# Threshold attention and a SoLU feed-forward block on one core: other places for the loads of q, k and v, and one more place for weights times v

## The chip, the core and the metric

The kernel runs on one core of one Trainium2 chip. The metric is device time in microseconds (us); 13 executions of the kernel before had a median of 925.93 us, from 922.73 to 934.3. Five engines work side by side, each through its own list of instructions in order: TensorE (PE in the profile; PEld is its weight load), VectorE (DVE), ScalarE (ACT), GpSimd (POOL) and SyncE (SP), which issues DMAs. They wait for each other through semaphores.

## The reference

First an attention for 8 batches and 8 heads, with 576 rows of 64 columns each, in float32. Scores more than tau under their row's maximum are put out of play before the softmax:

```python
scores = scale * np.matmul(q, k.transpose(0, 1, 3, 2))
thresh = np.max(scores, axis=-1, keepdims=True) - tau
scores = np.where(scores >= thresh, scores, -1000000000.0)
scores = scores - np.max(scores, axis=-1, keepdims=True)
attn = np.exp(scores)
attn = attn / (np.sum(attn, axis=-1, keepdims=True) + 1e-09)
return np.matmul(attn, v).astype(np.float32)
```

Its result, seen as x with 4608 tokens of 512 columns, goes through a feed-forward block: `h = x @ w_in` (1024 columns), `solu = h * softmax(h)`, a layer norm of solu with gain `g_ln`, and `@ w_out` (back to 512 columns).

## The kernel before

The kernel is one long list that a Python loop writes at build time. The loop counts **rounds** (`rnd`). In the first 144 rounds (NS) each does one **slot**: the scores of 128 query rows for two heads, 18 slots per batch (PER = 18). Sixteen of the 18 are for the first 512 rows, two at a time for a pair of heads; the last two are for the 64 rows at the end ("ends") of every head. Rounds after 144 finish what is left.

**What a round holds, in the order in which it is written.** Loads due in this round (`load_at`); copies of finished output (`begin`); the turning of q and k pieces for later heads (`preps`, TensorE transposes of up to 7 pieces of 64 columns, copied out by ScalarE and VectorE) and the scores (line 391); the row maxima with tau (line 408, VectorE, twice a round); the ramp that drops what is under the threshold (line 419, ScalarE); the exponentials (line 428, ScalarE). Then, for the slot before, the division by the sum (line 438, GpSimd); the feed-forward's vector steps (`middle`); one feed-forward step on TensorE, and perhaps weights times v; the turning of the weights in 32 x 32 blocks for the slot before (line 450, VectorE), and after every second slot, in an even round, four DMAs that bring them into the order that TensorE needs (wT<-T, line 461); at last `late`, more feed-forward steps and the store of out (line 669).

**The scores' two PSUM tiles, s0 and s1,** are written anew each round, so TensorE can begin a round's scores only when the ramp and the copies of the round before have read them.

**Weights times v (PV,** `attend`, line 486) is due three rounds after the second slot of its pair. It takes one of two PSUM tiles, p0 and p1, which the feed-forward uses too. When the attention of 256 tokens is complete, two units of 128 tokens are put on the list `ready`.

**The feed-forward** of a unit takes four steps on TensorE, one a round: h halves 0 and 1 (line 540), later o halves 0 and 1 (line 642). `quarter` counts them: 0 and 1 are h of unit `cur`, 2 and 3 are o of the unit before it, `prev`. In quarter 2 the loop passes through an o step even where there is no `prev`; that round's step is then empty. After h half 1 (round n) come the maximum and exponential (n), the product (n+1), the statistics and norm (n+2), in the middle of round n+3 the **swap**, four DMAs from SP of 64 KB each that exchange 32-row groups between u and V (V<-u, line 620), and in round n+4 `ff_turn` on VectorE (uT<-V, line 630), which waits for the swap. The next round's row maxima stand behind `ff_turn` in VectorE's list.

**Where PV is placed** is decided by one condition, which lets it run beside no feed-forward step or an h step, never beside an o step:

```python
due = bool(pv_due) and pv_due[0][0] <= rnd
if due and (step is None or step[0] == "h") and len(pairs_free) > (step == ("h", 0)):
    attending = pv_due.pop(0)[1]
```

**Loads.** A batch's q, k and v come in halves of four heads. `load_qk` loads q and k of a half (512 KB each) and with half 0 the ends of all heads (two DMAs of 128 KB); `load_v` loads v of a half in five DMAs, once in order (512 KB), once with the two halves of the partitions exchanged (2 x 256 KB), and the last 64 rows twice (2 x 64 KB). For batch b > 1, with r = 18(b-1), they stand at the start of rounds r+2 (q and k, half 0), r+8 (half 1), r+9 (v, half 0) and r+24 (v, half 1); for batch 1 at 8, 12, 15 and 24. q and k have two buffers each, v three. All go through SP's queue, like the wT, swap and store DMAs, in the order in which they are written. SP waits for whatever the next DMA in its list needs, and the others stand behind it.

In the first 16 rounds the feed-forward's weights are loaded and decoded as well (`weight_load`, `weight_a`, `weight_b`, `weight_d`), in rounds 0, 2 and 4 whole pairs of heads are turned.

Of the kernel before, what the change touches and what calls it, by code (L numbers as in the profile page):

```python
# [8 lines left out]
F32 = mybir.dt.float32  # L9
# [7 lines left out]
P = 128  # L17
# [3 lines left out]
def kernel(  # L21
# [27 lines left out]
    nc = tc.nc  # L49
    B, H, S, D = q.shape  # L50
    DM, DFF = w_in.shape
    SM = 512
# [35 lines left out]
    NK = S // 64  # L88

    halves = {}  # L90
    ends = {}
# [6 lines left out]
    pairs_free = ["p0", "p1"]  # L98
# [17 lines left out]
        )  # L116


    def load_qk(b, hf):
        d = halves.setdefault((b, hf), {})  # L120
        hs = slice(4 * hf, 4 * hf + 4)

        if hf == 0:
            ends[b] = loads.tile([P, H, D], F32, tag="ends", name="ends")
        for nm, src, rows in (("q", q, ROWS[0]), ("k", k, ROWS[1])):
            d[nm] = loads.tile([P, 4, 4, D], F32, tag=nm, name=nm)

            parts = [slice(0, 2), slice(2, 4)] if b == 0 and hf == 0 else [slice(0, 4)]
            for x, part in enumerate(parts):
                queue = nc.scalar if nm == "k" and x + 1 < len(parts) else nc.sync  # L130
                queue.dma_start(
                    out=d[nm][:, part].rearrange("p h t d -> p h (t d)"),
                    in_=src[b, hs, 0:SM, :][part].rearrange("h (p t) d -> p h (t d)", t=4),
                )
                if hf == 0 and x == 0:
                    queue.dma_start(
                        out=ends[b][rows], in_=src[b, :, SM:S, :].rearrange("h p d -> p h d")
                    )

    def load_v(b, hf):  # L140
        d = halves.setdefault((b, hf), {})
        hs = slice(4 * hf, 4 * hf + 4)


        d["v"] = loads.tile([P, 4, NK, D], F32, tag="v", bufs=3, name="v")
        rest = v[b, hs, 0:SM, :].rearrange("h (p t) d -> p h (t d)", t=4)
        for to, rows, of in (
            (0, slice(0, P), slice(0, P)), (4, ROWS[0], ROWS[1]), (4, ROWS[1], ROWS[0])
        ):
            nc.sync.dma_start(  # L150
                out=d["v"][rows, :, to : to + 4].rearrange("p h t d -> p h (t d)"), in_=rest[of]
            )
        for rows in ROWS:
            nc.sync.dma_start(
                out=d["v"][rows, :, NK - 1], in_=v[b, hs, SM:S, :].rearrange("h p d -> p h d")
            )
# [285 lines left out]
    def blocks(s):  # L442
        b, kind, hp, r = slots[s]
        key = (b, kind, hp)
        if r == 0:
            units[key] = dict(T=work.tile([P, NB, 2, 2, 32], F32, tag="T", name="T"))
        u = units[key]
        T = u["T"]
        for h, w in enumerate(live.pop(s)["w"]):
            nc.vector.transpose(out=T[:, :, r, h, :], in_=w)  # L450
        if r == 0:
            return

# [222 lines left out]
    PER = NS // B  # L676
# [22 lines left out]
    load_at = {}  # L699
    for b in range(1, B):  # L700
        r = PER * (b - 1)

        for at, job, hf in zip(
            (2, 8, 9) if b > 1 else (8, 12, 15), (load_qk, load_qk, load_v), (0, 1, 0)
        ):
            load_at.setdefault(r + at, []).append(lambda b=b, job=job, hf=hf: job(b, hf))
        load_at.setdefault(r + PER + 6, []).append(lambda b=b: load_v(b, 1))

    with tc.manual_schedule():
        load_qk(0, 0)  # L710
        nc.scalar.dma_start(out=tau_t, in_=tau.partition_broadcast(P))
        constants()
        for x in range(3):
            weight_load(x)
        load_qk(0, 1)
        load_v(0, 0)
        nc.sync.dma_start(out=g_rows, in_=g_ln.rearrange("(c p) -> c p", p=P))
        whole_pair(0)
# [2 lines left out]

        pieces = {r: x for x, r in enumerate(range(16))}
        whole = {0: 1, 2: 2, 4: 3}
        load_at[3] = [lambda: load_v(0, 1)]

        ready = []
        rnd = 0
# [7 lines left out]
        while True:  # L735
            more = rnd < NS
            if not more and not (
# [1 line left out]
                or max([rnd - 1, *begin, *middle, *late]) >= rnd  # L739
            ):  # L740
                break
            for job in load_at.pop(rnd, []):
                job()
            for job in begin.pop(rnd, []):
                job()
            if rnd == NS:
# [39 lines left out]
            due = bool(pv_due) and pv_due[0][0] <= rnd  # L786
            step = None
            if quarter < 2 and cur is not None:
                step = ("h", quarter)
            elif quarter == 3:  # L790
                step = ("o", 1)
            elif not more:
                if between and ffn[between[0]].get("turned", NS + rnd) <= rnd:
                    prev = between.pop(0)
                    step = ("o", 0)
            elif quarter == 2 or (prev is not None and not due):
                if prev is None or (ffn[prev].get("turned", NS + rnd) <= rnd and w2_done):
                    step = ("o", 0)

            attending = None  # L800
            if due and (step is None or step[0] == "h") and len(pairs_free) > (step == ("h", 0)):
                attending = pv_due.pop(0)[1]
            if step == ("h", 0):
                ff_h(cur, 0, rnd + 1 < NS)
# [1 line left out]
            elif step == ("h", 1):  # L806
# [8 lines left out]
                at = rnd + 4 if more or not ready else rnd + 6  # L815
# [24 lines left out]
            if rnd - 1 in live:  # L840
                blocks(rnd - 1)
            for job in late.pop(rnd, []):
                job()
            if rnd == 3:
                gains()
            if rnd in pieces:
                x = pieces[rnd]
# [42 lines left out]
```

## Time and profile before

| | us |
|---|---|
| median of 13 executions | 925.93 |
| the profiled execution | 929.29 |
| its span (first to last instruction of the program) | 927.5 |
| TensorE busy | 858.1 (93%) |
| VectorE busy | 678.8 (73%) |
| ScalarE busy | 591.6 (64%) |
| GpSimd busy | 451.7 (49%) |
| a wT DMA (288 of 288 KB), issue to landing, median | 5.8 |
| a swap DMA (144 of 64 KB) | 4.0 |
| q and k loads (15 each of 512 KB) | 6.2 and 7.1 |
| v loads (16 of 512 KB) | 8.4 |
| all that the DMAs moved | 154.61 MB, 167 GB/s in the mean |

The profile is of one execution. Rows of engines in 40 slices give the busy share of each slice in tenths (9 is 90% or more); PEclk is the share of its full clock that TensorE was granted. In lists of waits a row says which engine and line waited for which, then the total in us, the number of times and the longest. In a timeline a row has start and duration in us, engine, line and operation, and in brackets how long the engine had been idle and what ended that; "issue" there means that the profile shows nothing that the engine waited for. "SPq" is SP issuing a DMA.

### The profile page before, as it was taken

How to read it: one execution, taken by the hardware profiler on the slowest of the kernel's cores; microseconds unless marked ns; L12 is line 12 of the kernel's file. 1: busy time of each engine (PE TensorE's matmuls, PEld its weight loads, DVE VectorE, ACT ScalarE, POOL GpSimd, SP SyncE). 2: the span in 40 equal slices, each digit the busy share in tenths (PEclk: the TensorE clock that was granted, in tenths of full speed). 3: DMA queues.
4: the chain of work that ended last, by engine and by line, in shares of the span. 5: the costliest groups of instructions: out<-in, count | busy, mean ns of one | idle time of the engine just before them, and what ended most of it. 6: DMA issues, size and time to landing. Idle time of an engine off the chain costs nothing. (4 is left out here: it accounts for less than half of the span.)

```text
span 927.5 us, 39657 instructions
## 1 busy us (share of the span) xinstructions
PE 858.1 (93%) x17089; PEld 623.5 (67%) x17089; DVE 678.8 (73%) x1306; ACT 591.6 (64%) x1240; POOL 451.7 (49%) x870
## 2 busy tenths in 40 slices
PE   5567779989899999999999999989999999999997
PEld 3335457868777777767777667866667777676555
DVE  5898967768867877767867777767867777877352
ACT  5766656767756766666767676757757677776121
POOL 2535545536555555545545555545545455655120
PEclk8778799999999999999999999999999999999999
DMA  8899868975879557975879557965878655866412
GB/s 255 202 246 254 188 133 190 234 173 127 181 167 225 129 133 179 232 160 133 187 148 226 129 130 181 228 143 129 187 171 209 139 130 128 189 144 143 91 47 47
DMA packets 95470, 154.61 MB, mean 167 GB/s; under 512 B 27192, under 2 KB 69184, under 8 KB 95296
## 3 DMA queue, kind: packets, MB, share of 16 engines
q1 hardware_dynamic: 93920, 150.12, 70.2%
q8 instruction: 134, 2.20, 1.0%
q10 hardware_dynamic: 1376, 1.97, 0.6%
q14 instruction: 40, 0.33, 0.1%
HBM read 46.14 MB, written 9.44 MB: 60 GB/s over the span
## 5 line engine op out<-in xcount | busy, mean ns | idle before, releaser
L408 DVE CUSTOM_DVE_ANT_0 w<-s_ps,tau_t 128x576 f32<-128x576 f32 x288 | 206.5, 754 | 154.3 <-PE s_ps L391 129.6
L419 ACT ACTIVATE w<-s_ps,nth 128x576 f32<-128x576 f32 x288 | 207.5, 743 | 122.2 <-DVE nth L408 98.4
L642 PE MATMUL o_ps<-w,uT 64*64 64x256 f32 x4608 | 272.1, 380 | 8.7 <-DVE uT L630 7.7
L642 PEld LDWEIGHTS o_ps<-w,uT 64*64 64x64 f32 x4608 | 218.1, 134 | 72.2 <-issue 24.4
L540 PE MATMUL h_ps<-w,xh 64*64 64x512 f32 x1856 | 221.6, 595 | 5.3 <-issue 5.3
L438 POOL TENSOR_SCALAR w<-w,sm 128x576 f32<-128x576 f32 x288 | 218.1, 769 | 14.3
L428 ACT ACTIVATE w<-w,ntau 128x576 f32<-128x576 f32 x288 | 220.3, 772 | 0.0
L450 DVE STREAM_TRANSPOSE T<-w 128x576 f32<-128x576 f32 x288 | 205.7, 750 | 4.4 <-POOL w L438 4.2
L486 PEld LDWEIGHTS pv<-wT,v 64*64 64x64 f32 x5760 | 171.0, 138 | 45.2 <-issue 25.4
L391 PE MATMUL s_ps<-kT,qT 64*64 64x64 f32 (+1 forms) x2048 | 174.2, 425 | 25.1 <-ACT w L419 22.8
L486 PE MATMUL pv<-wT,v 64*64 64x128 f32 (+1 forms) x5760 | 175.0, 266 | 10.1 <-DMA wT<-T 6.9
L540 PEld LDWEIGHTS h_ps<-w,xh 64*64 64x64 f32 x1856 | 111.6, 134 | 98.4 <-issue 68.0
L435 POOL TENSOR_SCALAR sm<-sm 128x2 f32<-128x2 f32 x144 | 35.7, 248 | 278.5 <-ACT w L428 275.7
L436 POOL TENSOR_TENSOR sm<-sm,mone 128x2 f32<-128x2 f32 x144 | 107.1, 744 | 12.0
L391 PEld LDWEIGHTS s_ps<-kT,qT 64*64 64x64 f32 x2048 | 64.4, 139 | 34.2 <-ACT w L419 28.9
L604 ACT ACTIVATE V<-u,nb,rs 128x1024 f32<-128x1024 f32 x36 | 44.7, 1241 | 53.3 <-POOL nb L594 53.3
L508 ACT COPY xh<-pv 128x256 f32<-128x256 f32 x64 | 23.9, 373 | 75.3 <-PE pv L486 75.3
L630 DVE STREAM_TRANSPOSE uT<-V 128x1024 f32<-128x1024 f32 x36 | 44.1, 1225 | 24.5 <-DMA V<-u 24.2
L428 ACT ACTIVATION_READ_ACCUMULATOR w<-w,ntau 128x1 f32 x288 | 57.0, 198 | 0.0
L562 ACT ACTIVATE u<-h_ps,hm 128x1024 f32<-128x1024 f32 x36 | 40.2, 1118 | 25.0 <-DVE hm L553 19.3
L553 DVE TENSOR_REDUCE hm<-h_ps 128x1 f32<-128x1024 f32 x36 | 43.0, 1194 | 14.0 <-PE h_ps L540 8.0
L568 DVE TENSOR_TENSOR u<-h_ps,u 128x1024 f32<-128x1024 f32 x36 | 42.8, 1189 | 10.4 <-ACT u L562 10.4
(74 smaller groups left out, 607.0 us busy)
## 6 DMA issues: line engine op xcount, KB each, us to landing
wT<-T SPq DMA_DIRECT2D x288, 288.0 KB, 5.8
V<-u SPq DMA_DIRECT2D x144, 64.0 KB, 4.0
out_dram<-ob SPq DMA_DIRECT2D x72, 128.0 KB, 2.8
v<-in_v_dram SPq DMA_DIRECT2D x16, 512.0 KB, 8.4
v<-in_v_dram SPq DMA_DIRECT2D x32, 256.0 KB, 7.7
q<-in_q_dram SPq DMA_DIRECT2D x15, 512.0 KB, 6.2
k<-in_k_dram SPq DMA_DIRECT2D x15, 512.0 KB, 7.1
raw<-in_moe_w_out_dram SPq DMA_DIRECT2D x8, 512.0 KB, 7.9
```

Of the source, the lines that this page charges most:

```text
L391: nc.tensor.matmul(out=ps[h][ROWS[y], ks], lhsT=lhsT, rhs=d["kT"][ROWS[h], ks], start=True, stop=True,)
L408: nc.vector.tensor_tensor_reduce(out=w, in0=ps[:, 0:S], in1=tau_t.to_broadcast([P, S]), scale=1.0, scalar=BIG, op0=ALU.add, op1=ALU.min, a ...
L419: nc.scalar.activation(out=d["w"][x], in_=d["ps"][x][:, 0:S], func=AF.Prelu, bias=d["nth"][x], scale=-1.0, alpha=1.0e30,)
L428: nc.scalar.activation(out=w, in_=w, func=AF.Exp, bias=ntau, scale=1.0, accum_out=sm[:, x : x + 1])
L436: nc.gpsimd.tensor_tensor(out=sm, in0=sm, in1=mone, op=ALU.pow)
L438: nc.gpsimd.tensor_scalar(out=w, in0=w, scalar1=sm[:, x : x + 1], scalar2=1.0, op0=ALU.mult, op1=ALU.mult)
L450: nc.vector.transpose(out=T[:, :, r, h, :], in_=w)
L486: nc.tensor.matmul(out=to, lhsT=d["v"][ROWS[u], h0 + h, m ^ 4 * u if m < 8 else m], rhs=rhs, start=m == 0, stop=m == NK - 1,)
L540: mm = nc.tensor.matmul(out=h[ROWS[y], f], lhsT=x[ROWS[r], c, ROWS[y]], rhs=w1_parts[ROWS[r], c, part ^ r], start=part == 0 and c == 0, st ...
L604: nc.scalar.activation(out=V, in_=u, func=AF.Identity, bias=nb, scale=rs)
L630: nc.vector.transpose(out=uT, in_=d["V"].rearrange("p y (m x) -> p m y x", x=32))
L642: nc.tensor.matmul(out=d["o"][ROWS[z], 512 * r : 512 * r + 256], lhsT=d["uT"][ROWS[r], m].rearrange("p y x -> p (y x)"), rhs=w2[ROWS[r], m ...
```

## The change

Two things change. First, each half's q, k and v are loaded in smaller portions, with a place of their own each: q and k apart (`load_one`), and v in two portions (`load_v` with `parts`: 0 is the 512 KB in order, 1 and 2 are the rest). For batch b > 1, with r = 18(b-1), the places are the ends of rounds r-1 (q, half 0), r+1 (k, half 0), r+7 (k, half 1), r+9 (q, half 1), r+11 and r+13 (v, half 0), r+21 and r+23 (v, half 1). For batch 1 they are 8, 7, 11, 12, 13, 15, 21 and 23. What is due in a round is now written behind the round's `late` steps and no longer ahead of everything; the load of batch 0's second half of v in round 3 moves with it. Whichever of q and k comes first for half 0 allocates the tile for the ends.

Second, up to round 39 PV may also run in a round whose feed-forward step is o half 1. It stands behind that step in TensorE's list.

```diff
-    def load_qk(b, hf):
+    def load_one(b, hf, nm, queue=None):
         d = halves.setdefault((b, hf), {})
         hs = slice(4 * hf, 4 * hf + 4)
-        if hf == 0:
-            ends[b] = loads.tile([P, H, D], F32, tag="ends", name="ends")
-        for nm, src, rows in (("q", q, ROWS[0]), ("k", k, ROWS[1])):
-            d[nm] = loads.tile([P, 4, 4, D], F32, tag=nm, name=nm)
...
+        src, rows = {"q": (q, ROWS[0]), "k": (k, ROWS[1])}[nm]
+        d[nm] = loads.tile([P, 4, 4, D], F32, tag=nm, name=nm)
+
+        parts = [slice(0, 2), slice(2, 4)] if b == 0 and hf == 0 else [slice(0, 4)]
+        for x, part in enumerate(parts):
+            queue = nc.scalar if nm == "k" and x + 1 < len(parts) else nc.sync
+            queue.dma_start(
+                out=d[nm][:, part].rearrange("p h t d -> p h (t d)"),
+                in_=src[b, hs, 0:SM, :][part].rearrange("h (p t) d -> p h (t d)", t=4),
+            )
+            if hf == 0 and x == 0:
+                if b not in ends:
+                    ends[b] = loads.tile([P, H, D], F32, tag="ends", name="ends")
                 queue.dma_start(
+                    out=ends[b][rows], in_=src[b, :, SM:S, :].rearrange("h p d -> p h d")
                 )
...
+    def load_qk(b, hf):
+        load_one(b, hf, "q")
+        load_one(b, hf, "k")
+
+    def load_v(b, hf, parts=(0, 1, 2)):
...
-        d["v"] = loads.tile([P, 4, NK, D], F32, tag="v", bufs=3, name="v")
+        if 0 in parts:
+            d["v"] = loads.tile([P, 4, NK, D], F32, tag="v", bufs=3, name="v")
...
-        for to, rows, of in (
-            (0, slice(0, P), slice(0, P)), (4, ROWS[0], ROWS[1]), (4, ROWS[1], ROWS[0])
+        for part, to, rows, of in (
+            (0, 0, slice(0, P), slice(0, P)), (1, 4, ROWS[0], ROWS[1]), (1, 4, ROWS[1], ROWS[0])
         ):
...
+            if part in parts:
+                nc.sync.dma_start(
+                    out=d["v"][rows, :, to : to + 4].rearrange("p h t d -> p h (t d)"),
+                    in_=rest[of],
+                )
-        for rows in ROWS:
+        for rows in ROWS if 2 in parts else ():
...
-        for at, job, hf in zip(
-            (2, 8, 9) if b > 1 else (8, 12, 15), (load_qk, load_qk, load_v), (0, 1, 0)
+        for at, job, hf, what in (
+            (-1 if b > 1 else 8, load_one, 0, "q"),
+            (1 if b > 1 else 7, load_one, 0, "k"),
+            (7 if b > 1 else 11, load_one, 1, "k"),
+            (9 if b > 1 else 12, load_one, 1, "q"),
+            (11 if b > 1 else 13, load_v, 0, (0,)),
+            (13 if b > 1 else 15, load_v, 0, (1, 2)),
+            (PER + 3, load_v, 1, (0,)),
+            (PER + 5, load_v, 1, (1, 2)),
         ):
-            load_at.setdefault(r + at, []).append(lambda b=b, job=job, hf=hf: job(b, hf))
-        load_at.setdefault(r + PER + 6, []).append(lambda b=b: load_v(b, 1))
+            load_at.setdefault(r + at, []).append(
+                lambda b=b, job=job, hf=hf, what=what: job(b, hf, what)
+            )
...
-        load_at[3] = [lambda: load_v(0, 1)]
+        load_at.setdefault(3, []).append(lambda: load_v(0, 1))
...
-            for job in load_at.pop(rnd, []):
-                job()
             for job in begin.pop(rnd, []):
...
-            if due and (step is None or step[0] == "h") and len(pairs_free) > (step == ("h", 0)):
+            fits = step is None or step[0] == "h" or (rnd < 2 * PER + 4 and step == ("o", 1))
+            if due and fits and len(pairs_free) > (step == ("h", 0)):
                 attending = pv_due.pop(0)[1]
...
             for job in late.pop(rnd, []):
                 job()
+            for job in load_at.pop(rnd, []):
+                job()
```

More of the change, by code (lines that the diff above doesn't have):

```diff
@@ L116, in sync @@
         )
-    def load_qk(b, hf):
+    def load_one(b, hf, nm, queue=None):
         d = halves.setdefault((b, hf), {})
         hs = slice(4 * hf, 4 * hf + 4)
-        if hf == 0:
-            ends[b] = loads.tile([P, H, D], F32, tag="ends", name="ends")
-        for nm, src, rows in (("q", q, ROWS[0]), ("k", k, ROWS[1])):
-            d[nm] = loads.tile([P, 4, 4, D], F32, tag=nm, name=nm)
-            parts = [slice(0, 2), slice(2, 4)] if b == 0 and hf == 0 else [slice(0, 4)]
-            for x, part in enumerate(parts):
-                queue = nc.scalar if nm == "k" and x + 1 < len(parts) else nc.sync
+        src, rows = {"q": (q, ROWS[0]), "k": (k, ROWS[1])}[nm]
[10 more added lines that the diff above has]
+                    ends[b] = loads.tile([P, H, D], F32, tag="ends", name="ends")
@@ L131, in load_qk @@
                 queue.dma_start(
-                    out=d[nm][:, part].rearrange("p h t d -> p h (t d)"),
-                    in_=src[b, hs, 0:SM, :][part].rearrange("h (p t) d -> p h (t d)", t=4),
-                )
[L135 to L140, printed above, removed]
+                    out=ends[b][rows], in_=src[b, :, SM:S, :].rearrange("h p d -> p h d")
+                )
@@ L141, in load_v @@
+    def load_qk(b, hf):
+        load_one(b, hf, "q")
+        load_one(b, hf, "k")
+    def load_v(b, hf, parts=(0, 1, 2)):
         d = halves.setdefault((b, hf), {})
         hs = slice(4 * hf, 4 * hf + 4)
-        d["v"] = loads.tile([P, 4, NK, D], F32, tag="v", bufs=3, name="v")
+        if 0 in parts:
+            d["v"] = loads.tile([P, 4, NK, D], F32, tag="v", bufs=3, name="v")
         rest = v[b, hs, 0:SM, :].rearrange("h (p t) d -> p h (t d)", t=4)
-        for to, rows, of in (
-            (0, slice(0, P), slice(0, P)), (4, ROWS[0], ROWS[1]), (4, ROWS[1], ROWS[0])
-        ):
-            nc.sync.dma_start(
-                out=d["v"][rows, :, to : to + 4].rearrange("p h t d -> p h (t d)"), in_=rest[of]
-            )
```

## The prediction

> **What bounds the kernel now.** I read the page first: TensorE is busy 93% and its clock is low only in the first fifth of the span.
>
> ```profile
> span 927.5 us, 39657 instructions
> PE 858.1 (93%) x17089; PEld 623.5 (67%) x17089; DVE 678.8 (73%) x1306; ACT 591.6 (64%) x1240; POOL 451.7 (49%) x870
> ...
> PE   5567779989899999999999999989999999999997
> ...
> PEclk8778799999999999999999999999999999999999
> DMA  8899868975879557975879557965878655866412
> ```
>
> So a gain has to come out of TensorE's roughly 69 us of idle time, or out of time at half clock. The list of waits says who causes them (total us, times, longest):
>
> ```profile
> DVE uT L630 <- DMA V<-u: 24.2, 13, 5.6
> ...
> PE o_ps L642 <- DVE uT L630: 7.7, 4, 3.4
> ...
> PE pv L486 <- DMA wT<-T: 6.9, 4, 3.2
> ```
>
> Then I put the timeline into rounds: line 408 runs twice a round, so its pairs date the rounds. From round 39 four rounds repeat, one unit's h half 0, h half 1, then another unit's o half 0, o half 1, with weights times v ("PV") beside both h halves. Windows of four rounds (us, then each engine's busy us and count, granted clock, DMA share, GB/s):
>
> ```profile
> 245.20:271.00 25.80, 23.73 (x518) 17.55 (x514) 16.29 (x31) 14.44 (x32) 12.34 (x25) 1.00 0.82 179
> 271.00:293.60 22.60, 22.60 (x477) 18.09 (x472) 17.73 (x35) 15.92 (x35) 11.95 (x25) 1.00 0.90 215
> 385.20:410.90 25.70, 23.59 (x493) 17.65 (x488) 17.84 (x37) 16.08 (x36) 11.95 (x24) 1.00 0.81 185
> 410.90:433.50 22.60, 22.60 (x476) 17.84 (x472) 17.87 (x35) 16.04 (x35) 12.08 (x25) 1.00 0.60 131
> 455.60:482.40 26.80, 24.93 (x516) 18.38 (x512) 17.36 (x31) 15.35 (x31) 13.00 (x27) 0.94 0.76 164
> 598.00:625.00 27.00, 24.40 (x489) 17.36 (x485) 17.96 (x37) 15.86 (x36) 11.63 (x24) 0.94 0.71 153
> 669.70:695.30 25.60, 23.48 (x516) 15.23 (x512) 17.35 (x31) 15.48 (x31) 13.01 (x27) 1.00 0.78 170
> ```
>
> A clean four takes 22.6 us with TensorE never idle; five fours take 25.6 to 27.0. In each of the five a bulk load stands in SP's queue shortly before a swap (V<-u). Round 63 to 64:
>
> ```profile
> 388.48 2.86 SPq L150 DMA_DIRECT2D v<-in_v_dram  x3
> 391.38 1.27 SPq L154 DMA_DIRECT2D v<-in_v_dram  x2
> 392.76 4.66 SPq L620 DMA_DIRECT2D V<-u  x4
> 399.71 1.25 DVE L630 STREAM_TRANSPOSE uT<-V 128x1024 f32<-128x1024 f32 x1 [3.98 <-DMA V<-u]
> 401.10 3.25 PE L642 MATMUL o_ps<-w,uT 64*64 64x256 f32 x56 [0.72 <-DVE uT L630]
> ```
>
> Five loads of v (1.1 MB) are issued just ahead of the swap; VectorE waits 3.98 us for it, in order, so the next round's row maxima, ScalarE behind them and TensorE are late. After the q and k load of round 74 the stall is different: TensorE gets no instructions.
>
> ```profile
> 465.58 0.20 PEld L540 LDWEIGHTS h_ps<-w,xh 64*64 64x64 f32 x7 [2.69 <-issue]
> ...
> 466.50:469.90 3.40, 3.40 (x31) 2.04 (x24) 0.60 (x1) 0.00 (x0) 1.89 (x3) 0.50 0.88 167
> ```
>
> The second line shows what follows: 3.4 us at clock 0.50.
>
> **What the Trainium skill says.** "DMA: Bandwidth & Descriptors", section "Queues, rings and completion order": each DMA engine takes descriptors in ring order, rings of other queues in turn. The trace agrees: the swap above lands only when v has. "Runtime: NRT & Kernel Launch", "Instruction fetch mechanics": instructions come in 16 KiB blocks through a DMA queue of their own, "mostly hidden". Here queue q8 moves 2.20 MB in 134 packets (16 KB each), and 2.69 us was not hidden. "TensorE: Matmul & The Clock Gate", "What's actually happening": idling a window of about 3.4 us halves the clock until a busy window has passed. The trace agrees (0.50 above, and after the idle stretches in rounds 16, 19, 28 and 100).
>
> **The change part by part.**
>
> *Loads.* The same 16 DMAs per batch, same bytes, same SP issues (0.6 to 1.9 us each); no compute instruction is added. Before, they come in lumps of 1.0 to 1.3 MB, at round 18(b-1) plus 2 (q, k half 0), 8 (q, k half 1), 9 (v half 0) and 24 (v half 1), each at the round's start. After, lumps of 0.5 to 0.64 MB stand at the end of odd rounds: plus -1 (q, half 0), 1 (k, half 0), 7 and 9 (k, q, half 1), 11 and 13 (v, half 0), 21 and 23 (v, half 1). Those that move later keep their margin: q of half 1 is turned from round 12 on and v of half 1 first read in round 26, two whole rounds (9 us or more) after their issue, against landings of 6.2 and 8.4 us in the table of issues; were one late, TensorE would wait the difference, some 2 us. I followed the loop by hand to see what stands next to them. The swap is in odd rounds nearly always (from round 76 in those that leave 3 over 4), in the middle, so a load at the end stands behind it and behind the store of out in SP's queue, where it used to stand before both; next comes wT in the even round, issued 3 to 4.5 us into it. At the 215 to 255 GB/s of busy stretches 0.6 MB takes 2.5 us, so it is through.
>
> Saving from round 39 on: the five fours 25.8 + 25.7 + 26.8 + 27.0 + 25.6 - 5 x 22.6 = 17.9 us; smaller excesses by the same subtraction (fours that begin in rounds 55, 79, 91, 95, 119) 0.4 + 0.9 + 0.6 + 1.0 + 1.4 = 4.3. Sum 22.
> Before round 39: in round 16 the swap stands behind v and VectorE waits 5.6 us; TensorE idles 3.4 and loses half of the 3.4 us at half clock that follow: 5.1. Round 30 waits 1.5 for wT, round 28 0.9 for instructions. Round 10 waits 2.9 for wT behind q and k; now q stands behind wT: 1.5. Sum 9.
>
> New SP waits: v half 1 takes the buffer of the previous batch's v half 0, whose last reader is the PV of that batch's row ends. By my walk it runs one round before the load, or in the same round (57, 75, 111). There SP waits until that PV ends, about one PV (2.2 us), and queued behind is only the wT of the even round, 3 us or more away. Cost nothing; if the cover went, up to 2.2 us three times.
>
> *PV in an o's second half, rounds below 40.* No work is added, only order. In the list of steps PV now falls in rounds 14, 18, 22, 26, 32 and 36 and is never overdue there; h and o run up to two rounds ahead, but two rounds without h or o come later (65, 74). From round 75 both kernels have identical steps, so the end is untouched and only the filling of thin rounds counts. TensorE's need per step, from rounds' durations: scores 0.85, h 3.4, o 3.5, PV 2.2, transposes 0.12 per piece.
> Before, thin rounds 14, 19, 28, 29, 38 last 6.7 + 6.3 + 6.5 + 4.8 + 4.5 = 28.8 and carry 1.5 + 3.5 + 3.5 + 3.6 + 3.1 = 15.2: 13.6 lost, less the 0.9 counted above, plus 1.3 of half clock in round 20: 14.0.
> After: round 14, VectorE-bound with the weight decoding, 6.7 - 3.05 = 3.7, its successor 0.4; round 27 has neither PV nor h or o, ScalarE needs 5.5 (ramps and exponentials 3.4, norm 1.24, copies) for 1.55 of TensorE work, 4.0; PV alone in 28, 65, 74: 1.7 + 1.7 + 1.5; h without PV in 19, 23, 29, 33, 37: rounds 21 and 31 show 4.6 against 4.2, so 2.0. Sum 15.0. An o half with PV is not in the trace: at least 4.5 + 2.2 = 6.7 us; above it wT may be late, whose margin in the nearest cases, PV two rounds after wT's issue, is mostly 2 to 3 us, so 0 to 2.3 (a load ahead of it) five times, 0 to 11 us; I take 1. Net 14 - 16 = a loss of 2.
>
> Sum: 22 + 9 - 2 = 29 us. A stall for instructions can come with any backlog, so I take 85%: 25 us. The profiled execution took 929.3 (span 927.5 and 1.8 around it) and becomes 904. The median, 925.9, is 3.4 lower, so a part of the stalls that I subtract was this execution's own; I take 24 from the median: **902 us**.
>
> **The rivals.**
> 1. *Half of it* (0.33). The smaller loads stand right behind wT in rounds without a swap, and backlog still meets instruction fetches. For: such waits follow q, k and v alike. Against: the clean four at 271.00 carries 215 GB/s. Half of 29: 908 to 920.
> 2. *wT late, slower* (0.05). The 25 PVs of every fourth round from 44 start 1.2 to 6.6 us (mostly 2 to 3) after wT's landing, as far as landings are known. If a load (2.5 us) stands ahead of wT, each could wait up to 1.3, and so could the five in an o half. It decides at 29/30 = 1.0 us each; at 1.3 the time is 926 - 29 + 39 = 936. Against: wT is issued 3 us or more into the even round.
> 3. *Hidden anyway* (0.04): SP reaches the new places just as early because it runs ahead of the engines, so transfers collide as before; 924 to 928. Against: the swap precedes the load in SP's order now, whatever SP's lead.
> 4. *More than counted* (0.05): each removed idle stretch also spares a half-clock window; 885 to 892.
>
> **How the numbers follow.** The likeliest, 0.53, is 892 to 908 with 902 inside. Eight in ten: 891 to 916, from most of rival 4's edge to two thirds of rival 1. A measurement of this kernel cannot tell 0.3% (2.8 us) from no change. Faster 0.53 + 0.33 + 0.05 = 0.91, same 0.04, slower 0.05.
>
> **What would show it.** Right: VectorE's wait for V<-u falls from 24.2 to under 6 us; the five fours come to about 22.6; the clock row stays at 9 after the first seven slices; round 27 is thin. Wrong: PV waits for wT over 10 us; TensorE's issue waits unchanged; swaps still issued behind loads (in SP's own list line 620 waits 7.0 us, six times, for v). The prediction fails if fetch stalls move rather than go, or if PV in an o half waits for wT.

## The result, and the profile after

The kernel after takes 910.54 us in the median (11 executions, 906.41 to 916.65) against 925.69 us for the kernel before on the same chips (48 executions). The ratio is 0.9848, 95% interval 0.9822 to 0.9873: 15.2 us faster. The forecast was 902 us, within 891 to 916. The direction and the range held; the likeliest case (892 to 908) was missed by 2.5 us.

The two profiled executions lie further apart than the medians: 929.29 and 907.58 us, 21.7. The page of the kernel after:

```profile
span 905.5 us, 39662 instructions
...
PE 852.7 (94%) x17089; PEld 670.5 (74%) x17089; DVE 678.2 (75%) x1306; ACT 591.7 (65%) x1240; POOL 451.6 (50%) x870
...
PE   5668799999999999999999999999999999999997
...
PEclk9667899999999999999999999999999999999999
DMA  8899886877777777876876777876876756766322
```

TensorE does the same 17089 matmuls. From the sixth slice to the last but one its row holds nothing but 9, where the row before had 7 and 8 for longer and again in between, and the DMA row, which used to swing between 5 and 9, lies mostly at 6 to 8. The deep swings are gone. Two rows from the list of waits of the kernel before (total us, times, longest):

```profile
PEld h_ps L540 <- issue: 75.6, 296, 3.0
...
PEld pv L486 <- issue: 25.4, 78, 2.6
```

The list of the kernel after:

```profile
PEld h_ps L545 <- issue: 43.0, 210, 2.1
...
PEld pv L491 <- issue: 22.3, 56, 4.7
...
DVE uT L635 <- DMA V<-u: 10.0, 10, 4.1
...
PE pv L491 <- DMA wT<-T: 8.6, 7, 3.8
```

VectorE's wait for the swap fell from 24.2 to 10.0 us. Of those 10.0, 6.0 lie behind round 135, where no load is left in either kernel, 4.1 of them in one wait at the very end. The kernel before has 5.7 us there too, so the part that loads could touch fell from 18.5 to 4.0 us. The waits marked "issue" became fewer as well. The timeline shows why the swap is waited for less. This is SP's list in rounds 65 to 67, with the v load that stood ahead of the swap in the lines of round 63 shown before, and then VectorE's line that waits for the swap:

```profile
395.25 3.36 SPq L625 DMA_DIRECT2D V<-u  x4
398.71 1.71 SPq L674 DMA_DIRECT2D out_dram<-ob  x2
400.46 0.59 SPq L154 DMA_DIRECT2D v<-in_v_dram  x1
401.16 4.03 SPq L466 DMA_DIRECT2D wT<-T  x4
```

```profile
401.98 1.25 DVE L635 STREAM_TRANSPOSE uT<-V 128x1024 f32<-128x1024 f32 x1 [0.97 <-DMA V<-u]
```

The swap is issued first, v behind it, and the wait is 0.97 us instead of 3.98. The v loads themselves land in 6.5 us (512 KB, median) instead of 8.4. But the windows of four rounds (us, each engine's busy us and count, granted clock, DMA share, GB/s) that begin in rounds 39, 63, 75, 99 and 111 did not all become clean:

```profile
246.66:269.91 23.25, 23.24 (x450) 18.49 (x453) 17.74 (x34) 15.74 (x34) 12.27 (x25) 1.00 0.78 172
382.73:404.73 22.00, 20.88 (x517) 17.73 (x512) 17.13 (x35) 15.66 (x35) 12.52 (x25) 1.00 0.74 180
...
445.18:469.16 23.98, 23.32 (x518) 17.58 (x514) 16.14 (x31) 14.39 (x32) 12.31 (x25) 1.00 0.73 171
582.83:605.36 22.53, 22.53 (x489) 18.11 (x485) 17.91 (x36) 15.89 (x36) 11.61 (x24) 1.00 0.73 176
...
650.09:674.49 24.40, 23.22 (x516) 16.99 (x512) 17.36 (x31) 15.36 (x31) 12.98 (x27) 1.00 0.73 169
```

The fours of 63 and 99 are short now (25.7 and 27.0 before), though TensorE still idles 1.1 us in the first. Those of 75 and 111 lie 1.4 and 1.8 us above 22.6, where the prediction took 4.2 and 3.0 to go, and in a second profiled execution of the same kernel 2.7 and 3.7 (25.25 and 26.29 us).

**Stages.** The same windows over whole stages, in us, from one profiled execution each. "Loads only" and "PV only" are experiments told below.

| rounds | before | after | after, again | loads only | loads only, again | PV only |
|---|---|---|---|---|---|---|
| 10 to 14 | 28.4 | 29.1 | 25.5 | 27.6 | 25.7 | 28.8 |
| 14 to 39 | 146.1 | 147.5 | 146.0 | 138.5 | 137.8 | 153.4 |
| 39 to 75 | 210.4 | 198.5 | 199.1 | 206.4 | 205.9 | 209.5 |
| 75 to 143 | 396.0 | 384.5 | 387.8 | 390.3 | 390.5 | 396.2 |
| behind 143 | 75.8 | 75.9 | 75.9 | 75.9 | 75.9 | 75.8 |

Rounds 14 to 39 did not gain at all in the kernel after, and 39 to 75 gained 11.9. That is the move of PV: 176 more of the recorded matmuls lie in rounds 14 to 39 (2980 against 2804) and 206 fewer in rounds 39 to 75 (4120 against 4326).

### The profile page after: what moved, and what is told of

Read it like the earlier page. It is cut to its first block, busy times and chain, and to the rows that moved or that the text cites. A ratio compares the mean times of both kernels' runs of the same rounds, so it can differ in the third digit from the quotient of the medians.

```text
span 905.5 us, 39662 instructions
## 1 busy us (share of the span) xinstructions
PE 852.7 (94%) x17089; PEld 670.5 (74%) x17089; DVE 678.2 (75%) x1306; ACT 591.7 (65%) x1240; POOL 451.6 (50%) x870
## 5 line engine op out<-in xcount | busy, mean ns | idle before, releaser
L647 PEld LDWEIGHTS o_ps<-w,uT 64*64 64x64 f32 x4608 | 236.9, 133 | 43.8 <-ACT xh L513 9.7
L545 PE MATMUL h_ps<-w,xh 64*64 64x512 f32 x1856 | 219.3, 589 | 1.8 <-issue 1.8
L455 DVE STREAM_TRANSPOSE T<-w 128x576 f32<-128x576 f32 x288 | 205.9, 751 | 5.5 <-POOL w L443 5.2
L491 PEld LDWEIGHTS pv<-wT,v 64*64 64x64 f32 x5760 | 176.6, 139 | 37.5 <-issue 22.3
L396 PE MATMUL s_ps<-kT,qT 64*64 64x64 f32 (+1 forms) x2048 | 178.8, 423 | 19.7 <-ACT w L424 17.2
L491 PE MATMUL pv<-wT,v 64*64 64x128 f32 (+1 forms) x5760 | 178.8, 268 | 10.6 <-DMA wT<-T 8.6
L545 PEld LDWEIGHTS h_ps<-w,xh 64*64 64x64 f32 x1856 | 125.6, 133 | 77.3 <-issue 43.0
L396 PEld LDWEIGHTS s_ps<-kT,qT 64*64 64x64 f32 x2048 | 70.6, 140 | 29.5 <-ACT w L424 25.1
```

The source lines that it names most:

```text
L396: nc.tensor.matmul(out=ps[h][ROWS[y], ks], lhsT=lhsT, rhs=d["kT"][ROWS[h], ks], start=True, stop=True,)
L491: nc.tensor.matmul(out=to, lhsT=d["v"][ROWS[u], h0 + h, m ^ 4 * u if m < 8 else m], rhs=rhs, start=m == 0, stop=m == NK - 1,)
L545: mm = nc.tensor.matmul(out=h[ROWS[y], f], lhsT=x[ROWS[r], c, ROWS[y]], rhs=w1_parts[ROWS[r], c, part ^ r], start=part == 0 and c == 0, st ...
L647: nc.tensor.matmul(out=d["o"][ROWS[z], 512 * r : 512 * r + 256], lhsT=d["uT"][ROWS[r], m].rearrange("p y x -> p (y x)"), rhs=w2[ROWS[r], m ...
```

## The experiments

My theory was that of the prediction: the new places of the loads carry the gain, PV's move about nothing. The rivals: PV's move helps or hurts by itself; the size of the portions does it, not the place; the q and k lumps cause the stalls for instructions, or something else does.

### Which part carries the gain

Loads only is the kernel after with the old condition for PV:

```diff
-            fits = step is None or step[0] == "h" or (rnd < 2 * PER + 4 and step == ("o", 1))
+            fits = step is None or step[0] == "h"
```

> The new places of all loads, with PV placed as before (never beside an o step). Theory (the loads carry the gain, PV's move is about neutral): ratio to the kernel before 0.980 to 0.988, 907 to 915 us against 925.7; VectorE's wait for V<-u under 12 us. Rival A (PV's new place carries it): 0.995 or more. Rival B (both are needed, because PV's move shifts the swaps by two rounds against the loads): 0.990 to 0.995.

PV only is the kernel before with the new condition:

```diff
-            if due and (step is None or step[0] == "h") and len(pairs_free) > (step == ("h", 0)):
+            fits = step is None or step[0] == "h" or (rnd < 2 * PER + 4 and step == ("o", 1))
+            if due and fits and len(pairs_free) > (step == ("h", 0)):
```

> PV also beside an o's second half below round 40, with all loads where they were. Theory: within 0.4% of before, since only the order of thin rounds changes. The swaps before round 65 then fall on other rounds than the q and k lumps of batch 3, so one stall of about 3 us may go or come. Rival A: 0.980 to 0.988. Its VectorE wait for V<-u stays over 18 us by the theory.

Loads only: 910.3 us, ratio 0.9806 (0.977 to 0.9841). PV only: 931.48 us, 1.0044 (1.0021 to 1.0066), slower. The loads carry all of it, and PV's move alone costs 4 us. The stages of PV only, rounds 14 to 39 and 39 to 75:

```profile
100.91:254.29 153.38, 141.23 (x3000) 107.44 (x3001) 111.51 (x223) 101.55 (x220) 76.92 (x147) 0.97 0.73 164
254.29:463.83 209.54, 201.22 (x4120) 151.82 (x4123) 158.23 (x309) 141.91 (x299) 108.61 (x212) 0.98 0.75 170
```

Rounds 14 to 39 take 7.3 us more than before and rounds 39 to 75 only 0.9 less, although 206 matmuls have left them: with the old loads TensorE idles 8.3 us there, with the new ones 2.3 (198.52 less 196.25 in the kernel after). So what PV's move pays in advance came back only where little else held TensorE up. With the new loads it pays 9.7 and gets back 7.4 by round 75 (after against loads only, again). Behind round 75, where both have the same steps, the kernel after is another 2.5 to 6.0 us shorter in its two profiled executions, nearly all of it in the fours that begin in rounds 75 and 111; why was not taken apart. By the ratios (0.9848, and 0.9795 in a later run, against 0.9806 and 0.9816) PV's move is about neutral.

### Place or size

The first experiment moves v of half 0 (all of its five DMAs) from the start of its round to the end, behind the swap, and leaves all else as before:

```diff
+        load_end.setdefault(r + (9 if b > 1 else 15), []).append(lambda b=b: load_v(b, 0))
...
+            for job in load_end.pop(rnd, []):
+                job()
```

> From the kernel before: one lump of v, half 0 of each batch, still whole (1.1 MB), moved from the start of its round to the round's end, behind the swap. Everything else as before. Theory 'place' (the swap waits for what stands ahead of it in SP's queue): the fours that begin in rounds 63 and 99 fall from 25.7 and 27.0 us to about 22.6 and round 16 from 10.7 to about 6.5, 8 to 12 us in all, ratio 0.987 to 0.992; VectorE's wait for V<-u 24 to about 12 us. Rival 'size' (the lump itself saturates the DMA engines wherever it stands): 0.997 to 1.003.

The second keeps it at the start, ahead of the swap, but splits it as the kernel after does:

```diff
+        for at, parts in ((9, (0,)), (11, (1, 2))):
+            load_at.setdefault(r + at + 6 * (b == 1), []).append(
+                lambda b=b, parts=parts: load_v(b, 0, parts)
+            )
```

> From the kernel before: v, half 0, cut in two portions (0.5 and 0.63 MB) at the starts of rounds r+9 and r+11 (batch 1: 15 and 17), so a portion still stands ahead of the swap in the fours that begin in rounds 63 and 99. Everything else as before. Theory 'place': a portion ahead delays the swap by about 2.5 us, of which some is hidden; the two fours keep a part of their stall, 23.5 to 25.5 us each, ratio 0.992 to 0.997, clearly less gain than the whole lump moved behind the swap (0.9894). Rival 'size': cutting is what helps, both fours come to about 22.6 and the ratio to 0.987 to 0.991, as good as behind the swap or better.

Behind the swap, whole: 917.25 us, 0.9894 (0.9855 to 0.9933). Ahead of the swap, split: 916.22 us, 0.9893 (0.9852 to 0.9934). The fours of 63 and 99, first of the whole load behind the swap:

```profile
386.55:409.85 23.30, 23.30 (x493) 17.46 (x489) 17.91 (x36) 16.42 (x36) 12.15 (x25) 1.00 0.71 182
595.81:620.11 24.30, 23.53 (x488) 16.09 (x484) 17.91 (x37) 17.09 (x37) 12.62 (x26) 1.00 0.82 187
```

then of the split load ahead of it:

```profile
373.12:397.80 24.68, 23.82 (x492) 16.37 (x488) 18.03 (x36) 16.53 (x36) 12.15 (x25) 1.00 0.80 190
...
585.07:607.95 22.88, 22.88 (x492) 16.35 (x488) 18.02 (x36) 16.11 (x36) 11.97 (x24) 1.00 0.86 199
```

Either suffices for about half of the gain. The place cuts VectorE's wait for the swap more (to 12.2 us against 17.3), so the prediction's mechanism is there; but it is not the only way to the same time, and the prediction argued from the place. The split is no pure test of size, though: one DMA of 512 KB is left ahead of the swap, and the other four go to a round without a swap.

What SP may issue belongs to this. In the kernel before, the swap's fourth DMA was issued at 396.91 us, just after the first v DMA had landed at 396.89, and the two DMAs of the store at 397.67 and 398.48, after the second and third (397.61 and 398.46). Each is the eighth behind the one that it follows. In all fourteen profiles no DMA of SP was issued before the one eight places ahead of it had landed, as far as landings are known. So five DMAs of v ahead of the swap also take places that its four need. Whether this limit is the chip's or that of the program as built was not tested.

### q and k

Only q and k get their new portions and places; v is as before.

> From the kernel before: q and k alone get their new places, one at a time; v's loads and PV stay. Theory: the fours that begin in rounds 39, 75 and 111, where the lump of q, k and ends stood two DMA groups ahead of a swap and of a block of TensorE's instructions, fall from 25.8, 26.8 and 25.6 us to 22.6 to 24, 6 to 10 us in all, ratio 0.989 to 0.994; v's stalls in rounds 16, 64 and 100 stay. Rival (q and k never mattered, v did): 0.998 to 1.002.

920.93 us, 0.992 (0.9889 to 0.9951). The wait for the swap stays (26.5 us), and so do the two fours that v spoils:

```profile
379.93:406.77 26.84, 24.95 (x493) 19.00 (x489) 17.94 (x36) 16.13 (x36) 11.97 (x24) 0.94 0.75 174
...
591.50:618.49 26.99, 24.48 (x488) 16.91 (x484) 17.94 (x37) 15.84 (x36) 11.62 (x24) 0.94 0.73 172
```

The fall to 22.6 to 24 us that I had expected for the fours of 39, 75 and 111 did not come: they take 24.2, 26.1 and 24.9. What q and k gain is spread: 0.5 to 1.7 us each in the fours that begin in rounds 14, 18, 39, 55, 75, 79, 91, 111 and 119, while those of 26, 30 and 63 take 0.5, 1.7 and 1.1 longer. The two savings, 1.06% for v's first half and 0.80% for q and k, make 1.86%, of loads only's 1.94%. They add as far as the intervals tell (each is 0.6 to 0.8% wide), which fits two separate causes.

### What is left when there are no loads

This kernel is loads only without the loads of batches 1 to 7; every batch is computed with batch 0's q, k and v, so only the transfers and their issuing are missing, no instruction of an engine that computes.

```diff
-            load_at.setdefault(r + at, []).append(
-                lambda b=b, job=job, hf=hf, what=what: job(b, hf, what)
-            )
+            pass
```

> The kernel with the new places of the loads and PV as before, but with the loads of batches 1 to 7 left out (35 MB); every batch computes with batch 0's q, k and v. It shows what loads can cost at most. Theory 1 (what is left after the change in the fours that begin in rounds 75 and 111, 27.0 and 26.9 us, is a stall for TensorE's instructions that does not come from loads but from the dense list of PV for the row ends, 144 matmuls with their weight loads, followed by h and a PV): both fours stay over 25 us and the ratio is 0.970 to 0.980. Theory 2 (loads near by cause it): both fall to about 22.6 and the ratio is 0.960 to 0.970.

The lines show only the core of the edit; the places that look up q, k and v ask for batch 0's. 907.74 us, 0.9783 (0.974 to 0.9826), against 0.9806 with the loads. By the medians the new places have taken out nearly all that loads cost here, all but some 2 us (0.23%), with intervals that overlap almost wholly. The fours of 75 and 111 in its profiled execution:

```profile
444.67:471.24 26.57, 24.62 (x518) 18.86 (x513) 17.36 (x31) 15.27 (x31) 12.95 (x27) 0.94 0.51 112
...
653.13:676.48 23.35, 23.23 (x517) 17.90 (x513) 17.38 (x32) 15.38 (x31) 13.06 (x27) 1.00 0.57 126
```

The first takes 26.57 us (26.80 before, with all loads in lumps), with the DMA engines busy for 0.51 of the time. The second takes 23.35, and TensorE is busy in all but 0.12 of it. I had expected both to stay over 25, so this half failed: without loads the stall of round 76 is whole, in round 112 TensorE hardly idles, and there the loads have a share, as far as one profile tells. These 23.35 us are also what such a four takes with no stall, 0.7 more than the 22.6 from which the prediction subtracted. The timeline of this kernel in round 76:

```profile
455.12 0.20 PEld L545 LDWEIGHTS h_ps<-w,xh 64*64 64x64 f32 x8 [2.83 <-issue]
455.12 1.70 PE L545 MATMUL h_ps<-w,xh 64*64 64x512 f32 x12 [1.95 <-issue]
```

This is the stall that the prediction showed from the kernel before, 2.69 us in the same place, and there is no q or k load that could cause it. The DMA records tell what it is: the stall ends 2.5 us after a 16 KB packet of queue q8 begins to move (452.61 to 455.12). In the kernel before it is 2.6 us (462.96 to 465.58), in loads only, again, 2.5 (448.78 to 451.27), and in round 112 of the kernels before, after and loads only 2.5 to 2.7. So these stalls are fetches of instructions, and once begun a fetch takes as long without loads as with them. It begins too late. In this kernel the fetch before it lies 11.6 us back, and TensorE had executed some 530 instructions in between.

The loads are not what filled the DMA engines ahead of this fetch. SP's issue of wT around the start of round 75, and the whole stretch from the first of these transfers to the fetch (us, each engine's busy us and count, granted clock, DMA share, GB/s):

```profile
444.39 3.51 SPq L466 DMA_DIRECT2D wT<-T  x4
445.50:452.50 7.00, 7.00 (x201) 5.19 (x194) 4.63 (x10) 5.04 (x10) 5.08 (x8) 1.00 0.89 192
```

The first line is from the timeline, the second from the windows. The DMA engines are idle from 442 to 445 us and then busy for a share of 0.89 of these 7.0 us, mostly with wT, whose third DMA lands at 452.12; the packet begins to move at 452.61. That it waited for wT is suggested by this order and not shown, as no run changed wT's transfers.

### Moving the work that stands ahead of the stall

What distinguishes these rounds is PV of the row ends in round 75 and in round 111: 144 matmuls of 64 columns with their weight loads in about 2.4 us, beside h half 0, followed by h half 1 and the next PV. The edit is made to loads only, with one more permission: above round 40 PV of row ends may stand beside o half 1. That moves two PVs by a round each, from 75 to 74 and from 111 to 110, and nothing else.

```diff
             fits = step is None or step[0] == "h"
+            if due and step == ("o", 1) and rnd > 40:
+                fits = pv_due[0][1][1] == 2
```

> The new places of the loads, PV as before except that, above round 40, PV of the row ends may also run beside an o's second half. Only two PVs move: batch 3's from round 75 to 74 and batch 5's from 111 to 110, so the dense list stands one round further from the next h and PV. Theory 1 (density of instructions): the fours that begin in 75 and 111 lose their stall in rounds 76 and 112; with one PV less in the four they come to 20 to 21 us (from 27) while those that begin in 71 and 107 grow by 2 to 3 us; 6 to 9 us less in all than with the loads alone, ratio to before 0.971 to 0.976. Theory 2 (loads): the stalls stay, ratio 0.979 to 0.984.

Beside it, on the same chip, the kernel after once more:

> The changed kernel once more, beside the others on one chip, as the mark to beat: ratio 0.982 to 0.987. The kernel with the loads alone had 0.9806 on another chip; if PV's new place costs what it costs by itself (0.44%), this one is slower than the loads alone by 1 to 5 us.

Then this kernel again, with loads only beside it, on another chip:

> The row-ends kernel once more, beside the loads-only kernel on the same chip. If its gain over loads only comes from the stalls that it takes out of rounds 76 and 112, it is again 4 to 9 us under loads only, the four that begins in round 75 and the one in round 111 take 20 to 21 us each and the fours ahead of them (71 and 107) 24 to 25.5. If the earlier difference was one of chips, the two are within 2 us.

> Loads only, for comparison on this chip: 908 to 911 us, ratio near 0.981; the fours of rounds 75 and 111 take 26 to 27 us.

First time: 903.75 us, 0.9764 (0.9713 to 0.9814), and on the same chip the kernel after, again, 907.33 us, 0.9795 (0.9752 to 0.9838). Second time: 905.86 us, 0.976 (0.9725 to 0.9794), and on the same chip loads only, again, 912.48 us, 0.9816 (0.9772 to 0.9859). The intervals of each pair still overlap; twice in the same direction, by 3.6 and 6.6 us. Where the second pair differs, in the fours that begin in rounds 71, 75, 107 and 111; first loads only, again:

```profile
418.94:441.01 22.07, 22.07 (x436) 17.51 (x432) 17.86 (x35) 15.96 (x34) 11.72 (x23) 1.00 0.82 193
441.01:468.11 27.10, 24.93 (x516) 18.37 (x512) 17.36 (x31) 15.37 (x31) 12.99 (x27) 0.94 0.66 153
...
627.64:649.71 22.07, 22.07 (x437) 19.05 (x433) 17.89 (x35) 15.96 (x34) 11.72 (x23) 1.00 0.87 192
649.71:676.43 26.72, 24.93 (x517) 18.33 (x513) 17.37 (x32) 15.37 (x31) 13.07 (x27) 0.94 0.68 156
```

then with the row ends' PV moved:

```profile
416.94:442.88 25.94, 24.45 (x581) 19.60 (x576) 17.95 (x36) 16.95 (x36) 14.45 (x28) 1.00 0.83 186
442.88:463.10 20.22, 20.22 (x372) 15.67 (x368) 16.87 (x32) 14.18 (x30) 9.81 (x21) 1.00 0.73 178
622.49:648.40 25.91, 24.63 (x580) 19.63 (x576) 17.96 (x35) 16.94 (x36) 14.45 (x28) 1.00 0.85 185
648.40:668.62 20.22, 20.22 (x372) 15.67 (x368) 16.87 (x31) 14.19 (x30) 9.79 (x21) 1.00 0.73 178
```

The pairs of fours, 49.17 and 48.79 us, become 46.16 and 46.13, and no half clock is left in them. In the second four of each TensorE is never idle; the first keeps 1.3 to 1.5 us; shorter stalls for instructions now stand in rounds 74 and 110 (1.6 and 1.0 us on the weight loads). The move makes the stalls smaller and shifts what is left of them.

**Both at once.** The kernel without loads with the same edit:

> Leaves out the loads of q, k and v of batches 1 to 7 (all batches are computed with batch 0's) and lets the row ends' PV run beside o half 1 above round 40. If loads and the density of PV are two separate causes, the two savings add: the kernel without loads gives up another 4 to 7 us, 901 to 904 us, and rounds 76 and 112 show no stall for instructions. If the move of the row ends' PV only made room for the loads, it is worth nothing here: 906 to 908 us, as without loads alone.

901.54 us, 0.97 (0.9669 to 0.9731), against 0.9783 without loads alone. The moved PV is worth 0.8% here, where there is nothing to make room for, and 0.56% in the pair above: two separate causes, as far as the intervals tell. Its fours that begin in rounds 71 and 75:

```profile
420.62:444.79 24.17, 24.17 (x580) 19.41 (x576) 17.86 (x35) 16.99 (x36) 13.45 (x27) 1.00 0.60 128
444.79:465.02 20.23, 20.23 (x372) 15.55 (x368) 16.83 (x32) 14.25 (x30) 10.79 (x23) 1.00 0.59 139
```

TensorE is busy in all of their 44.4 us. That is what the pair costs without a stall; the kernel before took 48.9. The causes meet in one place: the stall of round 74 that the row-ends kernel keeps with the loads (the fetch begins at 437.77 us, as wT and a load of k issued at 431.64 come to their end) is not here.

### One more step, and what it doesn't settle

The row-ends kernel with PV also beside o half 1 in rounds 33 and 37, which gives the thin round 38 an h step and makes round 66 thin instead:

```diff
-            if due and step == ("o", 1) and rnd > 40:
-                fits = pv_due[0][1][1] == 2
+            if due and step == ("o", 1) and (rnd > 40 or rnd in (33, 37)):
+                fits = rnd <= 40 or pv_due[0][1][1] == 2
```

> The row-ends kernel with PV also beside o half 1 in rounds 33 and 37, so that the thin round 38 gets an h step and a thin round 66 comes in its place. If thin rounds cost what they carry too little, wherever they stand, this changes nothing: within 1.5 us of the row-ends kernel. If a thin round costs less behind round 40, where nothing is decoded any more, rounds 14 to 39 grow less than rounds 39 to 75 shrink and it is 2 to 5 us faster. If an o half with PV makes wT late, it is 2 us or more slower.

903.41 us, 0.973 (0.9698 to 0.9762), beside 905.86 for the row-ends kernel on the same chip: 2.4 us less, with intervals that overlap by more than half. In the profiled executions rounds 14 to 39 take 3.7 us more (143.57 against 139.90) and rounds 39 to 75 3.7 less (204.96 against 208.65). So the traces favour "a thin round costs the same wherever it stands", and the 2.4 us are not told from nothing. Of the kernels that have all of the computation in them it has the lowest ratio, 0.973, where the change as made gives 0.9848 and, once more, 0.9795.

## Why the prediction was right, and where it was wrong

**Loads before round 39: 9 us forecast.** Right in the sum. Loads only saves 7.6 and 8.2 us in rounds 14 to 39, where 7.5 were forecast. Round 16 alone went from 10.70 to 6.16 us in the kernel after, 4.5 of the 5.1 forecast. The 1.5 us for round 10 can't be judged: rounds 10 to 14 took between 25.1 and 30.7 us over all the executions profiled, whatever was changed. Some of the agreement is luck: at most 0.7 of the 1.5 us of round 30 went (the four that begins there takes 22.04 us before, 21.99 and 21.37 in loads only), since TensorE waits for wT there without any load too (2.0 us), and 1.5 to 1.7 us came from the four that begins in round 18, which the prediction had not put down to loads.

**Loads from round 39 on: 22 us forecast.** Here the sum failed. Loads only saves 10.0 us in rounds 39 to 143 (606.4 to 596.4). Term by term, before against loads only, again:

| fours | forecast | measured |
|---|---|---|
| 63 and 99 (v ahead of the swap) | 3.1 + 4.4 = 7.5 | 2.82 + 4.34 = 7.2 |
| 75 and 111 (stall for instructions) | 4.2 + 3.0 = 7.2 | -0.3 - 1.1 = -1.4 |
| 39 (stall for instructions in round 40) | 3.2 | 0.7 |
| 55, 79, 91, 95, 119 | 4.3 | 2.9 |

The failed step is the one that says "After the q and k load of round 74 the stall is different: TensorE gets no instructions", and then adds this four, 111's and 39's to the loads' account all the same. The difference was seen and not priced. A load that stands near a stall in SP's list is no proof that it causes it: the stalls of rounds 76 and 40 come without any load (2.8 and 1.9 us), and two PVs moved by one round each take those of 76 and 112 away, and leave at most 1.6 us two rounds earlier. Only in round 112 did the kernel without loads lose the stall. Those three fours are 11 us of the 12 that were missing.

**PV's move: a net loss of 2 us forecast.** About right with the new loads up to round 75: 9.7 paid, 7.4 got back, a loss of 2.3. Round 27 is thin as forecast: TensorE is busy in 3.44 of its 6.36 us (5.11 us in the second execution). What the prediction did not see is that the sum depends on the loads: with the old ones it loses 4 us. Nor did it see that the move brings the row ends' PV from round 39 to 38 and that the stall of round 40 goes with it (from 1.9 to 2.4 us in loads only to 0.2), so that the four of 39 falls to 23.25 us after all, by the other half of the change (23.79 in PV only).

**The 85% and the 24 us from the median.** The factor was meant for stalls "with any backlog". That fits what stayed: in round 76 no load was needed, the backlog of wT was there. But 15% was too little for it. Of 29 us worked out, the traces show 21.7, the medians 15.2. The kernel after's profiled execution was 3.0 us under its median and that of before 3.6 above its own, which is the whole difference; the prediction took 1 us of it into account.

**Edits costed at nothing.** Right. SP's own list shows one wait of a v load for TensorE, of 0.6 us, and line 625 no longer waits for a v load in it. PV's waits for wT rose only from 6.9 to 8.6 us, under the 10 set as the point where the forecast would be wrong.

**The marks that were set.** "VectorE's wait under 6 us" was set wrongly: 10.0, and 11.0 in the kernel without any loads. Most of the part that loads cause is gone; the rest belongs to the swap itself, above all behind round 135, where the kernel before already waits 5.7 us. "The five fours about 22.6": two of five, with a third at 23.25. "The clock row at 9 after the seventh slice": held, but the row before shows 9 from its sixth slice on as well, so this mark could tell nothing. "TensorE's issue waits unchanged": they fell, on h from 75.6 to 43.0 us. "The prediction fails if fetch stalls move rather than go": those of rounds 76 and 112 stayed where they were (1.4 to 3.0 us in two executions, 2.7 and 3.0 before), and a new one of 1.7 to 1.8 us came in round 21, which PV only has too.

**The reading of the clock.** The prediction says that the trace agrees with the page that it names: idling a window of about 3.4 us halves the clock. It agrees less than that. In the 3.41 us before the clock fell in round 76 of the kernel before, TensorE was busy for 1.54 us, and before the half clocks of rounds 19, 28 and 100 for 1.2 to 1.6, so here it took no wholly idle stretch of that length.

**The rivals.** The number fell into "half of it" (908 to 920), but not by the reason given: it put the missing half down to the smaller loads behind wT and to their backlog. Without loads the time is only some 2 us lower than with them, so the loads do not hold such a half; where a backlog meets the fetch of round 76, it is wT's own. That the range held is thus in part luck: its upper end rested on this rival. "wT late", "hidden anyway" and "more than counted" did not come.

## What to carry to other kernels

A stall that a transfer precedes has to be tried without the transfer before its time is put down to it: one kernel without the loads, its work otherwise the same, gave the bound for all moves of loads. Here the short transfer that VectorE waits for was helped by being put ahead of a bulk load in SP's list, and as much by leaving only a part of that load ahead of it. And work that is moved forward to fill thin places is paid at once; here it came back only where the stage that it left had little else to wait for.

## What the hardware showed that I had not expected

The instruction packets of queue q8 are TensorE's: 134 packets of 16 KB in every execution. "Runtime: NRT & Kernel Launch", section "Instruction fetch mechanics", of the Trainium skill has 256 instructions in each block, which makes 34,304; TensorE has 17,089 matmuls and as many weight loads, 34,178, and some 250 semaphore instructions. The stalls lie on this grid. Over all fourteen profiles the weight loads have 49 idle stretches of over 1 us between rounds 39 and 143 that the profile marks "issue". Counting TensorE's instructions from 0, 43 of them end at one whose number leaves 193 or 194 when divided by 256. The other six stand in rounds 46, 64 and 100, where the swap was late.

The page calls the crossing from one block to the next "mostly hidden". The traces agree for most of the 134, and show one to four stalls of over 1 us behind round 39 in every profile but that of PV only, which has eight. They end 2.2 to 3.1 us after the packet begins to move, with loads and with none, and the packet itself takes 0.9 to 1.6 us. Two things go with them. One is dense work ahead of the crossing: where PV of the row ends stands in round 39, 75 or 111, beside h half 0, the weight loads stand still for 1.35 to 3.06 us in the round after it, in every profile but for round 112 without loads (1.0); where it stands in round 38, 74 or 110, rounds 40, 76 and 112 have no such stretch over 0.4. The other is what fills the DMA engines. In the kernel before, from round 39 to 143, a packet that began after a microsecond with fewer than two of the 16 DMA engines busy came when TensorE still had 240 instructions to do before it came to the next place on the grid (median of 21, at least 155); after one with more than twelve busy it had 153 (median of 65, down to 1). Without loads these are 247 (27 packets) and 153 (44), so late fetches go with the other transfers, wT's above all, as well. That full DMA engines cause the delay is argued from these records; no run tested it by changing wT's transfers. Round 30, where the row-ends kernels keep a wait of 2.4 to 2.8 us with and without loads, is another matter: it is off the grid, and TensorE's own wait there ends with wT.
